# Scaled scores copied out of the score banks, and the second unit's mask moved into the next step

## The chip, the cores and the metric

The kernel runs on one core of a Trainium2 chip. The metric is the device time of one execution in microseconds, the median of several runs.

## The reference

Three layers follow each other, all in float32: a sparse attention (4 batches, 8 heads, 576 tokens, head dimension 64), a gated feed-forward layer (512 to 1536 and back), and a second one with a softmax-like activation and a layer norm (512 to 1024 and back). The change concerns the attention alone:

```python
scores = scale * np.matmul(q, k.transpose(0, 1, 3, 2))
thresh = np.max(scores, axis=-1, keepdims=True) - tau
scores = np.where(scores >= thresh, scores, -1000000000.0)
scores = scores - np.max(scores, axis=-1, keepdims=True)
attn = np.exp(scores)
attn = attn / (np.sum(attn, axis=-1, keepdims=True) + 1e-09)
return np.matmul(attn, v).astype(np.float32)
```

## The kernel before, in words

**Stages.** `attention` runs first, `moe1` (the gated layer, three matmuls for each product of float32 split in two parts) second, `moe2` third. While the attention runs, weights of the second stage are loaded and converted from float64 in pieces: six operations a piece, one on ScalarE (L121), three on VectorE (L125, L128, L131), one on ScalarE (L135), one on GpSimd (L138). The functions `fill` and `conv_emit` place them one by one into the steps.

**Units.** The heads are taken in 16 pairs. A pair has nine units of 128 rows of scores by 576 columns: units 0 to 7 are the four blocks of 128 queries of each of the two heads, unit 8 holds the last 64 queries of both heads, and its scores take twice as many matmuls. A score tile `ps` fills two banks of PSUM, 288 columns in each; the pool `ps_s` has two such tiles.

**What a unit goes through.** `scores` (L277): matmuls into `ps`. `soft_max` (L283): VectorE reads `ps`, multiplies by minus the scale and takes the minimum along the row, `nm`; the elementwise result goes to `junk`, which nobody reads. `soft_exp` (L295): ScalarE reads `ps` again and writes exp(scale * score + nm) to `pe` (unit 8: `pet`). `soft_thr` (L300): GpSimd makes the threshold `th` from `nm` and tau. `soft_mask` (L309): VectorE reads `ps` a third time, compares it with `th`, multiplies into `pe` in place, and sums the row into `z`. One step later `tpose` (L329) transposes the masked unit on TensorE into a tile `tp`, and ScalarE evacuates it (L322). Later `pv` (L360) multiplies with V in four halves per pair, two of 256 and two of 322 columns. `tpose_tail` (L345, L348) transposes the last 64 columns into another tile `tq` of the tag `tp`, `finish` (L381) the reciprocals of the row sums, also into a tile of that tag; it has three buffers. ScalarE evacuates that one into `zt` (L386), and P·V into `xp` (L368).

**The order of the work** is written out by hand. Each engine takes its instructions in the order in which the program issues them. The loop over `m` takes two units a step, A and B (`cur`), and those of the step before (`old`). The string `PROG`, 'ABtVFTUYaufbz', gives the order: A and B are scores, maximum and exponential of the two units; t and u the thresholds; V the P·V matmuls that are due; F `finish`; T and U the transposes of the two old units; Y their tails; a and b the masks; f and z fillers (reciprocals of row sums in `lo_old`, then weight conversions). At the end of the step come DMAs and ScalarE's evacuations: P·V and `zt` first, then those of T, U and Y, then weight conversions. Nine units against two a step make the pattern repeat every nine steps, two pairs. One step of nine has no P·V matmuls; one has both a `finish` and a tail. The last units are in step 71; steps 71 and 72 begin with `prep_x`, which prepares the first block of the second stage on VectorE (L199 and L202).

A score tile comes free when the mask has read it, so scores of a step wait for the masks of the step before:

```python
nc.tensor.matmul(ps[rows, g, 0:HS], lhsT=q[r, u, c], rhs=k[r, u, o:o + HS], start=True, stop=True, skip_group_check=True)
...
nc.vector.scalar_tensor_tensor(out=pv, in0=ps[:, :, 0:HS], scalar=th, in1=pv, op0=ALU.is_ge, op1=ALU.mult, accum_out=z[:, s:s + 1])
```

Of the kernel before, what the change touches and what calls it, by code (L numbers as in the profile page):

```python
# [8 lines left out]
F32 = mybir.dt.float32  # L9
F32R = mybir.dt.float32r  # L10
BF16 = mybir.dt.bfloat16
U32 = mybir.dt.uint32
U64 = mybir.dt.uint64
AF = mybir.ActivationFunctionType
ALU = mybir.AluOpType
AX = mybir.AxisListType
PSUM = bass.MemoryType.PSUM
P = 128
# [3 lines left out]
def kernel(  # L22
# [11 lines left out]
    nc = tc.nc  # L34
    NP, _, VS, D = v.shape
# [11 lines left out]
    HS = S // 2  # L47
# [9 lines left out]
    SCALE = 1.0 / float(D) ** 0.5  # L57
    BIG = 3.0e38
    EPS = 1e-9
    NS = 2 * NQ + 1  # L60
# [11 lines left out]
    taub = const.tile([P, 1], F32, name="taub")  # L72
    neg = const.tile([P, 1], F32, name="neg")
    toff = const.tile([P, 1], F32, name="toff")
# [144 lines left out]

    def tau_consts():  # L220
        nc.vector.tensor_scalar(out=neg, in0=taub, scalar1=0.0, scalar2=None, op0=ALU.is_lt)
        nc.vector.tensor_scalar(out=taub, in0=taub, scalar1=-1.0 / SCALE, scalar2=None, op0=ALU.mult)
        nc.vector.scalar_tensor_tensor(out=toff, in0=neg, scalar=BIG, in1=taub, op0=ALU.mult, op1=ALU.add)

    def attention():
        es = ExitStack()
# [2 lines left out]
        pp = es.enter_context(tc.tile_pool(name="pp", bufs=3))  # L229
# [5 lines left out]
        st = {}  # L235
# [42 lines left out]
            st[i, s] = ps  # L278

        def soft_max(i, s, nm):  # L280
            ps = st[i, s]
            junk = pp.tile([P, 2, HS], BF16, name="junk", bufs=1)
            nc.vector.tensor_scalar(out=junk, in0=ps[:, :, 0:HS], scalar1=-SCALE, scalar2=None, op0=ALU.mult, op1=ALU.min, accum_out=nm)  # L283
            st[i, s] = (ps, nm)

        def soft_exp(i, s):
            ps, nm = st[i, s]
            if s < 2 * NQ:
                qc, h = divmod(s, 2)
                if h == 0:  # L290
                    st[i, "p", qc] = pp.tile([P, 2, S], F32, name="pe", bufs=4)
                pe = st[i, "p", qc][:, h]
            else:
                pe = pp.tile([P, S], F32, name="pet", bufs=2)
            nc.scalar.activation(out=pe.rearrange("p (g s) -> p g s", g=2), in_=ps[:, :, 0:HS], func=AF.Exp, bias=nm, scale=SCALE)  # L295
            st[i, s] = [ps, pe, nm]

        def soft_thr(nm):
            th = sm.tile([P, 1], F32, name="th")
            nc.gpsimd.tensor_scalar(out=th, in0=nm, scalar1=-1.0 / SCALE, scalar2=toff, op0=ALU.mult, op1=ALU.add)  # L300
            return th

        def soft_mask(i, s, th):
            ps, pe, _ = st[i, s]
            if s == 0:
                st[i, "z"] = sm.tile([P, NS], F32, name="z", bufs=2)
            z = st[i, "z"]
            pv = pe.rearrange("p (g s) -> p g s", g=2)
            nc.vector.scalar_tensor_tensor(out=pv, in0=ps[:, :, 0:HS], scalar=th, in1=pv, op0=ALU.is_ge, op1=ALU.mult, accum_out=z[:, s:s + 1])  # L309
            st[i, s] = pe  # L310

        def recip(i):
            rz = sm.tile([P, NS], F32, name="rz", bufs=2)
            z = st[i, "z"]
            lo_q.append(lambda: nc.vector.tensor_scalar(out=rz, in0=z, scalar1=EPS, scalar2=None, op0=ALU.add))
            lo_q.append(lambda: nc.vector.reciprocal(out=rz, in_=rz))
            st[i, "rz"] = rz
# [98 lines left out]
                        conv_emit(wstage, "APD", 2)  # L416

        conv_at = [x for x in range(6, tot // 2 + 6) if x % 2 == 0 or x >= tot // 2]
        PROG = 'ABtVFTUYaufbz'
        for m in range(tot // 2 + 6):  # L420
            if m == tot // 2 - 10:
                load_x(0)
# [2 lines left out]
            cur = [divmod(n, NS) for n in (2 * m, 2 * m + 1) if n < tot]  # L425
# [4 lines left out]
            nm = {}  # L430
            th = {}
# [9 lines left out]
                if k < len(cur):  # L441
                    th[k] = soft_thr(nm[k])

            def mask(k):
                if k < len(cur):
                    soft_mask(*cur[k], th[k])
                    if cur[k][1] == NS - 1:
                        recip(cur[k][0])

            def turn(k):  # L450
                if k < len(old):
                    tpose(*old[k])

            for ch in PROG:
                if ch in "AB":
                    score("AB".index(ch))
                elif ch == "V":
                    for mm in mms:
                        mm()
                elif ch == "F":  # L460
                    for j in range(NP):
                        if m - j * NS // 2 == 9:
                            finish(j)
                elif ch in "TU":
                    turn("TU".index(ch))
                elif ch == "Y":
                    for c in old:
                        tpose_tail(*c)
                elif ch in "tu":
                    thr("tu".index(ch))  # L470
                elif ch in "ab":
                    mask("ab".index(ch))
                elif ch == "f":
                    fill(1)
                elif ch == "z":
                    fill(max(1, len(lo_old)))
# [4 lines left out]
            i, s = divmod(2 * m, NS)  # L481
# [312 lines left out]
```

## Time and profile before

| what | value |
| --- | --- |
| median of 3 runs | 994.72 us (992.99 to 995.31) |
| the profiled execution: its own time | 994.94 us |
| the profiled execution: span from first to last instruction | 993.2 us |
| mean granted TensorE clock | 0.997 |
| TensorE matmuls busy | 958.6 us, 97% of the span |
| VectorE busy | 552.1 us, 56% |
| ScalarE busy | 461.8 us, 47% |
| GpSimd busy | 196.1 us, 20% |

The page counts an engine as busy while one of its instructions executes; in the views below PE is TensorE's matmuls, PEld its weight loads, DVE is VectorE, ACT is ScalarE, POOL is GpSimd. Times are microseconds from the start of the span, those of single instructions in group views nanoseconds. "[1.15 <-DVE pe L309]" behind an instruction says that its engine stood idle for 1.15 us before it and what ended the wait. The shares are means over three stages: the attention fills about the first third of the span, and only there are VectorE and ScalarE busy for most of the time.

### The profile page before, as it was taken

How to read it: one execution, taken by the hardware profiler on the slowest of the kernel's cores; microseconds unless marked ns; L12 is line 12 of the kernel's file. 1: busy time of each engine (PE TensorE's matmuls, PEld its weight loads, DVE VectorE, ACT ScalarE, POOL GpSimd, SP SyncE). 2: the span in 40 equal slices, each digit the busy share in tenths (PEclk: the TensorE clock that was granted, in tenths of full speed). 3: DMA queues.
4: the chain of work that ended last, by engine and by line, in shares of the span. 5: the costliest groups of instructions: out<-in, count | busy, mean ns of one | idle time of the engine just before them, and what ended most of it. 6: DMA issues, size and time to landing. Idle time of an engine off the chain costs nothing.

```text
span 993.2 us, 17033 instructions
## 1 busy us (share of the span) xinstructions
PE 958.6 (97%) x6464; PEld 797.9 (80%) x6464; DVE 552.1 (56%) x1262; ACT 461.8 (47%) x889; POOL 196.1 (20%) x294
## 2 busy tenths in 40 slices
PE   6999898999899999999999999999999999999997
PEld 3555555555558999999999999999999788888885
DVE  5888888877887665553222666322322544444443
ACT  4777777777775444443222444211221434333332
POOL 1111112111113311220000333000001233333331
PEclk9999999999999999999999999999999999999999
DMA  5423532432615655444210554222102111111100
GB/s 140 143 85 96 157 103 84 132 96 82 165 59 176 204 169 155 142 134 122 92 49 24 179 156 154 72 73 72 47 26 94 32 50 47 46 49 45 44 22 32
DMA packets 56002, 95.59 MB, mean 96 GB/s; under 512 B 15088, under 2 KB 33648, under 8 KB 55920
## 3 DMA queue, kind: packets, MB, share of 16 engines
q1 hardware_dynamic: 55488, 93.91, 31.0%
q8 instruction: 51, 0.84, 0.4%
q10 hardware_dynamic: 432, 0.59, 0.2%
q14 instruction: 31, 0.25, 0.1%
HBM read 70.80 MB, written 23.68 MB: 95 GB/s over the span
## 4 chain that ended last, share of the span: by engine, by line
PE 83%; DVE 10%; issue 2%; ACT 2%; DMA 1%; POOL 1%; SPq 0%; DVEq 0%; ACTq 0%
PE ps L542 29%; PE py L564 15%; PE po L698 10%; PE ps L646 9%; PE ps L277 7%; PE po L360 7%; PE tp L329 5%; DVE junk L283 3%; DVE pe L309 2%; PE pl L679 1%; DVE pet L309 1%; PE tq L345 1%; DMA wraw<-in_w_dram 1%; DMA k<-in_qkv_dram 1%; DVE w L131 0%
## 5 line engine op out<-in xcount | busy, mean ns | idle before, releaser
L542 PE MATMUL ps<-xt,w 128*128 128x288 f32 x2304 | 321.4, 295 | 0.3 <-DVE g L549 0.2
L542 PEld LDWEIGHTS ps<-xt,w 128*128 128x128 f32 x2304 | 310.9, 188 | 0.7 <-DVE g L549 0.7
L564 PE MATMUL py<-gt,w 128*128 128x288 f32 x1152 | 168.1, 295 | 0.0
L564 PEld LDWEIGHTS py<-gt,w 128*128 128x128 f32 x1152 | 158.0, 188 | 0.0
L549 DVE TENSOR_TENSOR g<-ps,a 128x288 f32<-128x288 f32 x96 | 43.8, 457 | 192.7 <-ACT a L548 192.7
L138 POOL TENSOR_TENSOR w<-w,w 128x512 fp32r<-128x512 f32 x52 | 77.9, 1498 | 289.9 <-ACT w L135 289.9
L283 DVE TENSOR_SCALAR_CACHE_REDUCE junk<-ps 128x576 bf16<-128x576 f32 x144 | 109.0, 757 | 43.2 <-PE ps L277 34.5
L277 PE MATMUL ps<-k,q 64*128 64x288 f32 (+1 forms) x640 | 105.8, 450 | 25.7 <-DVE pe L309 15.8
L548 ACT ACTIVATE a<-ps 128x288 f32<-128x288 f32 x96 | 39.3, 409 | 187.3 <-PE ps L542 187.3
L295 ACT ACTIVATE pe<-ps,nm 128x576 f32<-128x576 f32 x128 | 94.8, 743 | 66.3 <-DVE junk L283 65.3
L698 PE MATMUL po<-w,lt 128*128 128x512 f32 x432 | 104.5, 395 | 2.6 <-ACT lt L684 1.3
L309 DVE SCALAR_TENSOR_TENSOR pe<-ps,th,pe 128x576 f32<-128x576 f32 x128 | 104.0, 816 | 5.0 <-POOL th L300 3.2
L646 PE MATMUL ps<-w,ys 128*128 128x512 f32 x432 | 105.2, 398 | 1.3 <-POOL ys L518 1.3
L698 PEld LDWEIGHTS po<-w,lt 128*128 128x128 f32 x432 | 80.4, 187 | 23.6 <-ACT lt L684 2.2
L277 PEld LDWEIGHTS ps<-k,q 64*128 64x128 f32 (+1 forms) x640 | 47.3, 179 | 62.3 <-issue 26.4
L646 PEld LDWEIGHTS ps<-w,ys 128*128 128x128 f32 x432 | 79.6, 187 | 20.3 <-POOL ys L518 1.7
L322 ACT ACTIVATE pt<-tp 128x512 f32<-128x512 f32 (+1 forms) x160 | 79.0, 552 | 7.7 <-PE tp L329 5.8
L300 POOL TENSOR_SCALAR th<-nm,toff 128x1 f32<-128x1 f32 x144 | 38.1, 265 | 216.3 <-DVE junk L283 214.2
L360 PE MATMUL po<-pt,vr 128*64 128x322 f32 (+1 forms) x512 | 78.3, 427 | 0.1
L329 PEld LDWEIGHTS tp<-ident,pe 128*128 128x128 f32 x512 | 58.0, 145 | 24.8 <-issue 17.4
L329 PE MATMUL tp<-ident,pe 128*128 128x128 f32 x512 | 72.9, 285 | 0.9 <-ACT pt L322 0.9
L551 DVE TENSOR_TENSOR gt<-g,gt 128x288 fp32r<-128x288 f32 x96 | 44.0, 458 | 49.1 <-ACT gt L550 49.1
(73 smaller groups left out, 802.3 us busy)
## 6 DMA issues: line engine op xcount, KB each, us to landing
wraw<-in_w_dram SPq DMA_DIRECT2D x36, 512.0 KB
q<-in_qkv_dram SPq DMA_DIRECT2D x15, 576.0 KB
k<-in_qkv_dram SPq DMA_DIRECT2D x30, 176.0 KB
xd<-xp SPq DMA_DIRECT2D x16, 289.0 KB
xr<-xd SPq DMA_DIRECT2D x8, 576.0 KB
zr<-rzd SPq DMA_DIRECT2D x16, 288.0 KB
xsd<-xr SPq DMA_DIRECT2D x8, 576.0 KB
ypd<-y SPq DMA_DIRECT2D x8, 576.0 KB
```

What stands on the lines that cost most here:

```text
L138: nc.gpsimd.tensor_tensor(out=w["o"][1], in0=w["f"] if wide else raw, in1=w["o"][0].bitcast(F32), op=ALU.subtract)
L277: nc.tensor.matmul(ps[rows, g, 0:HS], lhsT=q[r, u, c], rhs=k[r, u, o:o + HS], start=True, stop=True, skip_group_check=True)
L283: nc.vector.tensor_scalar(out=junk, in0=ps[:, :, 0:HS], scalar1=-SCALE, scalar2=None, op0=ALU.mult, op1=ALU.min, accum_out=nm)
L295: nc.scalar.activation(out=pe.rearrange("p (g s) -> p g s", g=2), in_=ps[:, :, 0:HS], func=AF.Exp, bias=nm, scale=SCALE)
L309: nc.vector.scalar_tensor_tensor(out=pv, in0=ps[:, :, 0:HS], scalar=th, in1=pv, op0=ALU.is_ge, op1=ALU.mult, accum_out=z[:, s:s + 1])
L322: evac_q.append(lambda: nc.scalar.activation(out=out, in_=in_, func=AF.Copy))
L329: nc.tensor.transpose(tp[:, kc, :], pe[:, o:o + P], ident)
L360: nc.tensor.matmul(po[h * D:(h + 1) * D], lhsT=lhsT, rhs=rhs, start=(kc == 0), stop=(kc == NQ), skip_group_check=True)
L542: nc.tensor.matmul(pa[:, 0:NB], lhsT=wt[:, m, wi, kc * P:(kc + 1) * P], rhs=xt[:, kc, xi, :], start=(k == 0), stop=(k == 3 * KC - 1))
L564: nc.tensor.matmul(py, lhsT=wt[:, 2, wi, oc * P:(oc + 1) * P], rhs=gt[:, gi, :], start=(first and k == 0), stop=(last and k == 2))
L646: nc.tensor.matmul(ph[:, g, :], lhsT=y[:, a, kc, :], rhs=w2(2 * kc + g, b), start=(k == 0), stop=(k == 3 * KC - 1))
L698: nc.tensor.matmul(po, lhsT=lt[:, a, j, :], rhs=w2(2 * KC + j, b), start=(k == 0), stop=(k == 3 * NJ - 1))
```

## The change

`soft_max` writes its elementwise result, minus the scaled scores, as float32 to a tile `ns` in SBUF with four buffers, in place of `junk`. `soft_exp` and `soft_mask` read `ns`, so nothing but the maximum reads `ps`. The threshold is compared on the negative scaled scores, so the constants of `tau_consts` and the comparison turn round, and one operation on 128 x 1 elements goes. The order of a step becomes 'AtbBuVFTUYfaz': b, the mask of unit B, is put off into a list `late` and done in the next step, behind that step's first maximum and before its second. The first filler now stands ahead of mask A.

```diff
@@ -219,8 +219,7 @@
 
     def tau_consts():
         nc.vector.tensor_scalar(out=neg, in0=taub, scalar1=0.0, scalar2=None, op0=ALU.is_lt)
-        nc.vector.tensor_scalar(out=taub, in0=taub, scalar1=-1.0 / SCALE, scalar2=None, op0=ALU.mult)
-        nc.vector.scalar_tensor_tensor(out=toff, in0=neg, scalar=BIG, in1=taub, op0=ALU.mult, op1=ALU.add)
+        nc.vector.scalar_tensor_tensor(out=toff, in0=neg, scalar=-BIG, in1=taub, op0=ALU.mult, op1=ALU.add)
 
     def attention():
         es = ExitStack()
@@ -278,13 +277,12 @@
             st[i, s] = ps
 
         def soft_max(i, s, nm):
-            ps = st[i, s]
-            junk = pp.tile([P, 2, HS], BF16, name="junk", bufs=1)
-            nc.vector.tensor_scalar(out=junk, in0=ps[:, :, 0:HS], scalar1=-SCALE, scalar2=None, op0=ALU.mult, op1=ALU.min, accum_out=nm)
-            st[i, s] = (ps, nm)
+            ns = pp.tile([P, 2, HS], F32, name="ns", bufs=4)
+            nc.vector.tensor_scalar(out=ns, in0=st[i, s][:, :, 0:HS], scalar1=-SCALE, scalar2=None, op0=ALU.mult, op1=ALU.min, accum_out=nm)
+            st[i, s] = (ns, nm)
 
         def soft_exp(i, s):
-            ps, nm = st[i, s]
+            ns, nm = st[i, s]
             if s < 2 * NQ:
                 qc, h = divmod(s, 2)
                 if h == 0:
@@ -292,21 +290,21 @@
                 pe = st[i, "p", qc][:, h]
             else:
                 pe = pp.tile([P, S], F32, name="pet", bufs=2)
-            nc.scalar.activation(out=pe.rearrange("p (g s) -> p g s", g=2), in_=ps[:, :, 0:HS], func=AF.Exp, bias=nm, scale=SCALE)
-            st[i, s] = [ps, pe, nm]
+            nc.scalar.activation(out=pe.rearrange("p (g s) -> p g s", g=2), in_=ns, func=AF.Exp, bias=nm, scale=-1.0)
+            st[i, s] = (ns, pe)
 
         def soft_thr(nm):
             th = sm.tile([P, 1], F32, name="th")
-            nc.gpsimd.tensor_scalar(out=th, in0=nm, scalar1=-1.0 / SCALE, scalar2=toff, op0=ALU.mult, op1=ALU.add)
+            nc.gpsimd.tensor_scalar(out=th, in0=nm, scalar1=1.0, scalar2=toff, op0=ALU.mult, op1=ALU.add)
             return th
 
         def soft_mask(i, s, th):
-            ps, pe, _ = st[i, s]
+            ns, pe = st[i, s]
             if s == 0:
                 st[i, "z"] = sm.tile([P, NS], F32, name="z", bufs=2)
             z = st[i, "z"]
             pv = pe.rearrange("p (g s) -> p g s", g=2)
-            nc.vector.scalar_tensor_tensor(out=pv, in0=ps[:, :, 0:HS], scalar=th, in1=pv, op0=ALU.is_ge, op1=ALU.mult, accum_out=z[:, s:s + 1])
+            nc.vector.scalar_tensor_tensor(out=pv, in0=ns, scalar=th, in1=pv, op0=ALU.is_le, op1=ALU.mult, accum_out=z[:, s:s + 1])
             st[i, s] = pe
 
         def recip(i):
@@ -416,7 +414,8 @@
                         conv_emit(wstage, "APD", 2)
 
         conv_at = [x for x in range(6, tot // 2 + 6) if x % 2 == 0 or x >= tot // 2]
-        PROG = 'ABtVFTUYaufbz'
+        PROG = 'AtbBuVFTUYfaz'
+        late = []
         for m in range(tot // 2 + 6):
             if m == tot // 2 - 10:
                 load_x(0)
@@ -441,11 +440,10 @@
                 if k < len(cur):
                     th[k] = soft_thr(nm[k])
 
-            def mask(k):
-                if k < len(cur):
-                    soft_mask(*cur[k], th[k])
-                    if cur[k][1] == NS - 1:
-                        recip(cur[k][0])
+            def mask(c, t):
+                soft_mask(*c, t)
+                if c[1] == NS - 1:
+                    recip(c[0])
 
             def turn(k):
                 if k < len(old):
@@ -468,8 +466,14 @@
                         tpose_tail(*c)
                 elif ch in "tu":
                     thr("tu".index(ch))
-                elif ch in "ab":
-                    mask("ab".index(ch))
+                elif ch == "a":
+                    if cur:
+                        mask(cur[0], th[0])
+                    if len(cur) > 1:
+                        late.append((cur[1], th[1]))
+                elif ch == "b":
+                    while late:
+                        mask(*late.pop())
                 elif ch == "f":
                     fill(1)
                 elif ch == "z":

```

## Rows read from the trace of the kernel before

**Rows 1.** Busy time by stretch; behind the engines: granted TensorE clock, DMA share, GB/s.

```profile
235.00:240.00 5.00, 5.00 (x26) 3.14 (x26) 3.15 (x9) 2.92 (x6) 0.53 (x2) 0.66 0.00 0
...
400.00:600.00 200.00, 200.00 (x1508) 200.00 (x1507) 88.81 (x174) 73.12 (x157) 28.65 (x18) 1.00 0.36 115
```

**Rows 2.** Waits, 8 to 306 us: who waited for whom, total us, times, longest.

```profile
PE ps L277 <- DVE pe L309: 15.8, 20, 1.7
...
PE ps L277 <- DVE pet L309: 2.9, 8, 0.6
```

**Rows 3.** Timeline, step without P·V: start, us, engine, line, operation [idle before].

```profile
46.33 1.24 PE L277 MATMUL ps<-k,q 64*128 64x288 f32 x8
...
47.14 0.76 DVE L283 TENSOR_SCALAR_CACHE_REDUCE junk<-ps 128x576 bf16<-128x576 f32 x1 [1.11 <-PE ps L277]
...
47.94 0.74 ACT L295 ACTIVATE pe<-ps,nm 128x576 f32<-128x576 f32 x1 [0.88 <-DVE junk L283]
...
48.03 0.76 DVE L283 TENSOR_SCALAR_CACHE_REDUCE junk<-ps 128x576 bf16<-128x576 f32 x1
...
48.78 0.82 DVE L309 SCALAR_TENSOR_TENSOR pe<-ps,th,pe 128x576 f32<-128x576 f32 x1
...
49.75 0.76 PE L277 MATMUL ps<-k,q 64*128 64x288 f32 x4 [1.15 <-DVE pe L309]
```

**Rows 4.** Timeline of TensorE, L348 in steps with a `finish`, six cycles apart.

```profile
46.07 0.34 PE L348 MATMUL tq<-ident,pet 128*64 128x64 f32 x4
...
267.97 0.34 PE L348 MATMUL tq<-ident,pet 128*64 128x64 f32 x4
```

**Rows 5.** The chain that ended last, 66 to 83 us: start, us, what.

```profile
66.66 1.17 PE ps L277 x8
...
67.83 1.24 PE po L360 x8
...
69.06 1.02 PE tp L329 x8
...
71.65 1.78 PE po L360 x12
...
74.46 0.22 PE tq L345 x2
...
79.68 1.45 PE po L360 x12
```

**Rows 6.** Timeline of TensorE and ScalarE in a step with L381 and a tail.

```profile
79.61 1.08 PE L360 MATMUL po<-pt,vr 128*64 128x256 f32 x8
...
80.52 0.74 ACT L295 ACTIVATE pe<-ps,nm 128x576 f32<-128x576 f32 x1 [0.20 <-DVE junk L283]
...
81.48 0.25 ACT L386 ACTIVATE zt<-rt 9x128 f32<-9x128 f32 x1
...
82.05 0.38 PE L345 MATMUL tq<-ident,pe 128*128 128x128 f32 x2
```

**Rows 7.** Timeline of TensorE: a score pair whose first unit is split.

```profile
74.60 1.40 PE L277 MATMUL ps<-k,q 64*128 64x288 f32 x12
```

**Rows 8.** One source line each: ns min/median/max, first and last start (L138: 8 to 304 us).

```profile
L199 DVE SCALAR_TENSOR_TENSOR xr<-xr,vs,zr x32: 509/511/1565, 296.4 to 493.4; 128x288 f32<-128x288 f32 x32
...
L309 DVE SCALAR_TENSOR_TENSOR pe<-ps,th,pe x128: 808/817/820, 9.9 to 300.8; 128x576 f32<-128x576 f32 x128
...
L131 DVE SCALAR_TENSOR_TENSOR w<-w,wlow x52: 682/685/1593, 57.2 to 621.1; 128x512 uint32<-128x512 uint32 x52
...
L138 POOL TENSOR_TENSOR w<-w,w x12: 1267/1280/1284, 59.6 to 297.7; 128x512 fp32r<-128x512 f32 x12
```

**Rows 9.** Groups of ScalarE: busy us, mean ns of one, idle before, releaser.

```profile
L548 ACT ACTIVATE a<-ps 128x288 f32<-128x288 f32 x96 | 39.3, 409 | 187.3 <-PE ps L542 187.3
...
L550 ACT ACTIVATE gt<-g 128x288 fp32r<-128x288 f32 x96 | 42.7, 445 | 54.3 <-DVE g L549 54.3
```

**Rows 10.** Timeline of VectorE at the end of the attention.

```profile
302.44 1.42 DVE L202 TENSOR_TENSOR xt<-xr,xt 128x576 fp32r<-128x576 f32 x2
```

## The prediction

> **What bounds the kernel now.** I first asked for busy time by stretch. From 400 to 600 us TensorE is busy for the whole 200 us [rows 1], and so it is nearly to the end: what the change does to VectorE can win nothing in the two dense layers. The attention, about 8 to 307 us, is left. There I read the list of waits: TensorE sits 15.8 us on `pe` and 2.9 us on `pet`, both written by VectorE's mask at L309 [rows 2]. These are the score matmuls (L277), which need one of two score banks, and a bank is free only when its mask has read it. These 18.7 us are what the change is after.
>
> The timeline of one step without P·V matmuls shows the wait. Scores A start at 46.33, the first row maximum at 47.14 (0.81 later), the second at 48.03, mask A at 48.78, and the scores of the next step stand 1.15 us until that mask is through [rows 3]. VectorE goes maximum, maximum, mask, mask.
>
> The order repeats every nine steps (two head pairs). Its mark is the small tail matmul L348 in the step that also holds a `finish`: the one at 46.07 and the one at 267.97 are six cycles apart [rows 4], so a cycle takes 221.90 / 6 = 36.98 us, a step 4.11.
>
> **TensorE's own work in a cycle**, from pieces of the chain that stand without a wait: 1.17 for a score pair, 1.24 and 1.78 for the halves of the wide P·V, 1.45 for the second half of the narrow one, 1.02 for the two transposes, 0.22 for a tail [rows 5]; 1.08 for the narrow first half [rows 6]; 0.26 for L348, from 46.07 to 46.33 [rows 3, 4]; a score pair with the split last unit 1.40 less an overlap of some 0.06 [rows 7]. Sum: 7 x 1.17 + 2 x 1.34 + 2 x (1.08 + 1.45 + 1.24 + 1.78) + 9 x 1.02 + 4 x 0.22 + 2 x 0.26 = 32.55. So 4.43 us of a cycle are waits or slow matmuls. Part is the clock: between 235 and 240 the granted clock is 0.66 [rows 1]. Between the two levels of 2.4 and 1.2 GHz that is 68% of 5 us at the lower one, 1.7 us of work lost; one more such fall stands between 195 and 205, so 2 x 1.7 / 6 = 0.57 a cycle.
>
> **The change, part by part.**
>
> *Bank released by the maximum.* The exponential and the mask now read `ns`, so scores of the next step need only that a maximum is done, over 2 us earlier than TensorE comes to them. The bank waits go to nothing.
>
> *What is late next: mask B.* It is done in the next step between the two maxima, and the transposes of unit B stand behind it. From rows: maximum A starts 0.81 after the scores, the next operation of another kind 0.75 later (48.03 to 48.78), mask 0.82, and 0.15 to reach TensorE (mask A from 48.78 to 49.60, scores at 49.75) [rows 3]: 0.80 + 0.75 + 0.82 + 0.15 = 2.52. With a P·V half between, TensorE is at these transposes after 1.17 + 1.08 + 0.51 = 2.76 or later: hidden. In the one step of nine without P·V it is there after 1.68 and waits 0.84.
>
> *What is late as well: the exponential of B.* Maximum B now starts 2.29 after the scores instead of 1.70, its exponential 0.80 after that (47.14 to 47.94 for unit A [rows 3]), at 3.09. Behind it in ScalarE's queue stand the evacuations. In the one step of nine that has both the reciprocals' transpose (L381) and a tail, the tail takes a fourth buffer of `tp`, of which there are three, so it needs the evacuation `zt`. That starts 0.96 after the exponential and takes 0.25 [rows 6]: 3.09 + 0.98 + 0.25 + 0.15 = 4.47. TensorE would be there at 1.17 + 2.44 (79.61 to 82.05) = 3.61 and waits 0.86. Elsewhere the tail finds a buffer evacuated a step ago.
>
> *VectorE's own step*: four operations of alternating kinds at 0.75, 3.00, against 0.89 + 0.75 + 0.89 + 0.75 now, the second 0.89 being mask B's wait for its exponential (48.03 + 0.80 + 0.74 + 0.10 is 49.67, 0.89 after 48.78 [rows 3]). Three weight conversions (0.69 us each at most) for each of 12 pieces [rows 8] are 0.37 a step over 67 steps. 3.37 is under TensorE's 32.55 / 9 = 3.62, so what hides VectorE's work is thin, 0.25 a step.
>
> *Operations with another operand.* The maximum writes float32 instead of bfloat16: taken at nothing, at most the 0.06 by which a mask exceeds it, and hidden by that cover. The exponential reads SBUF: a ScalarE copy of 288 elements takes 445 from SBUF and 409 ns from PSUM [rows 9], so +0.04, in ScalarE's idle time except for the 0.02 that stand in the 0.98 above. The mask now has two SBUF sources. The nearest row is L199, the same kind of operation, float32, with a pointer scalar, two SBUF sources and no accumulator: 511 ns for 288 elements against 817 for 576 with one source in PSUM [rows 8]. That is 1.06 ns for each further element, one rate for both, so I take no change.
>
> The Trainium skill (Vector Engine (DVE) Microarchitecture Reference, section 7, Points that are easy to get wrong) says that this form with two SBUF sources that are not bfloat16 runs at half throughput, for want of a port for the accumulator. By that rule the sum would end slower, which is the third rival below; L199 with its 511 ns does not show it, but no row here has accumulator and two SBUF sources together.
>
> *Contention with GpSimd.* L199 and L131, with two SBUF sources, have maxima of 1565 and 1593 ns beside medians of 511 and 685; the mask with one in PSUM never exceeds 820 [rows 8]. The long ones stand beside a running L138 on GpSimd. After the change the mask is of the first kind, and 12 L138 fall into the attention. Each can cost from nothing to 1.05 us (1565 less 511): 0 to 12.6, taken at half of that, -6, since a held mask A has time to spare and a held mask B has little.
>
> *The threshold and the constants.* Same count on GpSimd; one tiny operation less before the first maximum, off the path: nothing. The reciprocal of odd pairs moves by a step and shifts weight conversions by a step; its reader is four steps away. No DMA moves past another on any queue.
>
> *Start.* The first three steps with transposes have no P·V either. Each can trade a wait like the 1.15 [rows 3] for the new 0.84, and the first may lose it whole: between 0 (K's arrival and slow first matmuls stand close behind) and 1.15 + 2 x 0.31 = 1.8, taken at +1.0.
>
> *End.* The last mask B now comes in a step that begins with two L202 subtractions (1.42 us [rows 10]), in front of it on VectorE; the last transposes and P·V wait for it. Between 0 and 3 with one conversion more in the last steps, taken at -1.2.
>
> **Sum.** A cycle falls from 36.98 to 32.55 + 0.84 + 0.86 + 0.57 = 34.82, by 2.16; steps 4 to 70 are 7.4 cycles: 16.0. 16.0 - 6 + 1.0 - 1.2 = 9.8. The profiled execution took 994.94, 0.2 above the median of 994.72; it gives 985.1, the median 984.9: I say 985.0.
>
> **The rivals.**
> 1. *The clock.* Both falls follow a step in which TensorE waited over a microsecond. The two new waits lie within some 5 us of each other in each cycle. If the clock falls in each, 7.4 x 1.7 = 12.6 instead of 4.2: +8.4, 993.4. For it: the falls. Against: most cycles have such waits now without a fall.
> 2. *GpSimd holds the masks.* Each L138 delays the path by its full 1.28, 15.4 instead of 6, with the next threshold queued behind it on GpSimd: 994.4. For it: the 1565 ns. Against: L138 may meet mask A, which has slack.
> 3. *The mask at half rate* (slower): 576 x 1.06 = 0.61 us more for each mask. VectorE's step becomes 3.00 + 1.22 + 0.37 = 4.59, a cycle 41.3 instead of 36.98: +4.3 x 7.4 = 32, about 1027. It decides from the point where the step exceeds 4.11, 0.37 us more per mask. For it: the accumulator is new beside two SBUF sources. Against: L199.
>
> **How the numbers follow.** Forecast 0.72, rival 1 0.08, rival 2 0.08, rival 3 0.12. A measurement here can tell 0.2%, 2 us, from no change. The forecast is faster; rival 1 is half faster and half the same; rival 2 is 0.02 faster, 0.05 the same, 0.01 slower; rival 3 is slower. Faster 0.78, same 0.09, slower 0.13. The range goes down to 976, all 18.7 us of bank waits gained, and up to 993.5: the contention at its bound (+6.6) with the end at its bound (+1.8), which takes in rival 1 too. Rivals 2 and 3 and a remnant are left out.
>
> **What would show it.** Right: no TensorE wait on L309 before L277; cycles near 35.5; a wait of about 0.85 before unit B's transposes in the step without P·V and one on `zt` before L345; masks at 0.82 except beside L138. Wrong: a mask median near 1.4; the lower clock in each cycle; transposes waiting in steps with P·V, where mask B should be hidden.

## The result, and the profile after

The changed kernel takes 977.24 us (median of 4 runs, 976.68 to 977.84), the kernel before 993.93 (4 runs, 992.99 to 995.31): a ratio of 0.9831 [0.9814, 0.9848], 16.7 us less. The forecast was 985.0, from 976.0 to 993.5. The profiled execution took 976.86 us with a span of 975.1, so the two spans differ by 18.1 us where the working came to 9.8: the sign was right, and the size little more than half of what came. A second execution of the kernel before, profiled later, has a span of 991.7 us, 16.6 more than the changed kernel, which is the difference of the medians; what made the first longer is under *The clock*.

Part 5 of the page after, the groups of the attention:

```profile
L281 DVE TENSOR_SCALAR_CACHE_REDUCE ns<-ps 128x576 f32<-128x576 f32 x144 | 108.4, 752 | 35.3 <-PE ps L276 34.9
L293 ACT ACTIVATE pe<-ns,nm 128x576 f32<-128x576 f32 x128 | 98.6, 775 | 57.5 <-DVE ns L281 57.0
L298 POOL TENSOR_SCALAR th<-nm,toff 128x1 f32<-128x1 f32 x144 | 86.1, 600 | 154.7 <-DVE ns L281 144.6
L307 DVE SCALAR_TENSOR_TENSOR pe<-ns,th,pe 128x576 f32<-128x576 f32 x128 | 105.1, 821 | 5.4 <-POOL th L298 5.4
...
L276 PE MATMUL ps<-k,q 64*128 64x288 f32 (+1 forms) x640 | 95.7, 439 | 4.6 <-DMA k<-in_qkv_dram 4.6
```

The scores (now L276) wait for K's transfer at the very beginning and for nothing else: the 18.7 us of [rows 2] are gone. Before the maximum (L281) VectorE waits for TensorE. The mask takes 821 ns on average, the same as before [rows 8]; what has grown is a GpSimd operation on 128 x 1 elements, the threshold (L298), from a mean of 264 to 600 ns.

What TensorE waits for after, in the list of waits from 8 to 290 us (us in total, times, longest):

```profile
PE tq L343 <- ACT zt L384: 6.6, 8, 1.5
PE tp L327 <- ACT pe L293: 5.4, 8, 1.0
PE tp L327 <- DVE pe L307: 2.1, 2, 1.5
PE tp L327 <- DVE pet L307: 0.8, 1, 0.8
```

Two of these were forecast, each once in a cycle of nine steps. The timeline of the changed kernel shows one such place:

```profile
41.09 0.25 ACT L384 ACTIVATE zt<-rt 9x128 f32<-9x128 f32 x1
...
41.39 0.44 PE L343 MATMUL tq<-ident,pe 128*128 128x128 f32 x2 [0.53 <-ACT zt L384]
...
41.76 0.34 PE L346 MATMUL tq<-ident,pet 128*64 128x64 f32 x4
...
42.02 1.24 PE L276 MATMUL ps<-k,q 64*128 64x288 f32 x8
...
42.83 0.76 DVE L281 TENSOR_SCALAR_CACHE_REDUCE ns<-ps 128x576 f32<-128x576 f32 x1 [1.98 <-PE ps L276]
...
43.20 0.66 PE L327 MATMUL tp<-ident,pe 128*128 128x128 f32 x4
...
43.51 0.82 DVE L307 SCALAR_TENSOR_TENSOR pe<-ns,th,pe 128x576 f32<-128x576 f32 x1
...
43.76 0.69 POOL L298 TENSOR_SCALAR th<-nm,toff 128x1 f32<-128x1 f32 x1 [2.79 <-DVE ns L281]
...
44.25 0.76 DVE L281 TENSOR_SCALAR_CACHE_REDUCE ns<-ps 128x576 f32<-128x576 f32 x1
...
44.48 0.63 PE L327 MATMUL tp<-ident,pe 128*128 128x128 f32 x4 [0.63 <-ACT pe L293]
...
45.04 1.24 PE L276 MATMUL ps<-k,q 64*128 64x288 f32 x8
...
248.55 0.34 PE L346 MATMUL tq<-ident,pet 128*64 128x64 f32 x4
```

The eight score matmuls of the next step now stand in one stretch of 1.24 us (45.04); before, they came as two groups of four, the first behind a wait of 1.15 [rows 3]. VectorE goes maximum (42.83), old mask B (43.51), maximum (44.25). TensorE waits until 44.48 for that mask, which ended at 44.33; the list names `pe` of ScalarE, which had long been done (the exponential in the same tile, 40.15 to 40.93), so the name is to be read with the timeline. From the mark at 41.76 to the one at 248.55 are six cycles: 206.79 / 6 = 34.47 us, against 36.98 [rows 4].

The busy time over six cycles splits that. First the changed kernel (stretch, its length, TensorE's matmuls busy, then weight loads, VectorE, ScalarE, GpSimd, granted clock, DMA):

```profile
41.76:248.55 206.79, 197.69 (x1501) 119.58 (x1500) 176.95 (x488) 162.33 (x310) 77.03 (x118) 1.00 0.39 118
```

then the same stretch of the fastest kernel of the study (with `ns`, old order of the masks, `finish` moved, below):

```profile
40.50:235.87 195.37, 195.37 (x1501) 119.64 (x1500) 177.45 (x486) 160.10 (x308) 41.01 (x118) 1.00 0.43 126
```

There TensorE has no gap at all: 195.37 / 6 = 32.56 us of work in a cycle; the forecast had 32.55 from single pieces. The changed kernel stands idle for 206.79 - 197.69 = 9.10 us, 1.52 a cycle (six waits on `zt` of 4.5 us together, six for mask B of 4.6), and its matmuls take 197.69 - 195.37 = 2.32, or 0.39 a cycle, longer. 32.56 + 1.52 + 0.39 = 34.47.

### The profile page after: what moved, and what is told of

It is laid out like the page before. It is cut to its first block, busy times and chain, and to the rows that moved or that the text cites. A ratio compares the mean times of both kernels' runs of the same rounds, so it can differ in the third digit from the quotient of the medians.

```text
span 975.1 us, 16895 instructions
## 1 busy us (share of the span) xinstructions
PE 948.0 (97%) x6464; PEld 798.6 (82%) x6464; DVE 539.7 (55%) x1261; ACT 460.2 (47%) x889; POOL 246.7 (25%) x294
## 4 chain that ended last, share of the span: by engine, by line
PE 90%; DVE 3%; ACT 2%; issue 2%; DMA 1%; SPq 1%; POOL 0%; ACTq 0%; DVEq 0%
PE ps L546 31%; PE py L568 16%; PE po L702 10%; PE ps L650 9%; PE po L358 8%; PE ps L276 8%; PE tp L327 6%; PE pl L683 1%; ACT pe L293 1%; PE tq L343 1%; DMA q<-in_qkv_dram 1%; DVE pe L307 1%; DMA k<-in_qkv_dram 0%; PE tq L346 0%; DVE e L658 0%
## 5 line engine op out<-in xcount | busy, mean ns | idle before, releaser
L138 POOL TENSOR_TENSOR w<-w,w 128x512 fp32r<-128x512 f32 x52 | 80.7, 1553 | 282.7 <-ACT w L135 277.3
L281 DVE TENSOR_SCALAR_CACHE_REDUCE ns<-ps 128x576 f32<-128x576 f32 x144 | 108.4, 752 | 35.3 <-PE ps L276 34.9
L293 ACT ACTIVATE pe<-ns,nm 128x576 f32<-128x576 f32 x128 | 98.6, 775 | 57.5 <-DVE ns L281 57.0
L298 POOL TENSOR_SCALAR th<-nm,toff 128x1 f32<-128x1 f32 x144 | 86.1, 600 | 154.7 <-DVE ns L281 144.6
L307 DVE SCALAR_TENSOR_TENSOR pe<-ns,th,pe 128x576 f32<-128x576 f32 x128 | 105.1, 821 | 5.4 <-POOL th L298 5.4
L276 PE MATMUL ps<-k,q 64*128 64x288 f32 (+1 forms) x640 | 95.7, 439 | 4.6 <-DMA k<-in_qkv_dram 4.6
L276 PEld LDWEIGHTS ps<-k,q 64*128 64x128 f32 (+1 forms) x640 | 48.2, 178 | 29.1 <-issue 9.8
```

The costliest lines, as they stand in the source:

```text
L138: nc.gpsimd.tensor_tensor(out=w["o"][1], in0=w["f"] if wide else raw, in1=w["o"][0].bitcast(F32), op=ALU.subtract)
L281: nc.vector.tensor_scalar(out=ns, in0=st[i, s][:, :, 0:HS], scalar1=-SCALE, scalar2=None, op0=ALU.mult, op1=ALU.min, accum_out=nm)
L298: nc.gpsimd.tensor_scalar(out=th, in0=nm, scalar1=1.0, scalar2=toff, op0=ALU.mult, op1=ALU.add)
L307: nc.vector.scalar_tensor_tensor(out=pv, in0=ns, scalar=th, in1=pv, op0=ALU.is_le, op1=ALU.mult, accum_out=z[:, s:s + 1])
```

## The experiments

**The two halves of the change.** First: `ns`, but the masks in the order of before.

```diff
-        PROG = 'AtbBuVFTUYfaz'
+        PROG = 'ABtVFTUYaufbz'
@@
-                    if len(cur) > 1:
-                        late.append((cur[1], th[1]))
                 elif ch == "b":
-                    while late:
-                        mask(*late.pop())
+                    if len(cur) > 1:
+                        mask(cur[1], th[1])
```

> Only the first half of the change: scaled scores in `ns`, but the order of a step as before (maximum, maximum, mask, mask, all in the unit's own step). Theory 1, the bank release carries the gain and the late mask opens two new waits (about 0.63 us on mask B in the step without P·V and 0.73 us on `zt` in the step with `finish` and tail, some 10 us in all): neither wait is there, VectorE's step is about 3.2 us (mask B waits for its exponential) plus 0.4 of fillers against TensorE's 3.6, so 972 to 982 us. Rival, the alternation is needed because VectorE's step would be the bound without it: 984 to 990 us, with score matmuls or transposes waiting on VectorE in most steps.

965.43 us (964.41 to 966.24), ratio 0.9713 [0.9695, 0.9731], less than either range expected; a cycle is 32.98 us. The copy outside the banks gains 28 us by itself, and moving the mask gives 12 of them back. TensorE's waits on `zt` shrink to 1.4 us in 3, and those for mask B in the step without P·V are gone.

Second: the mask moved, but read from the score banks as before.

```diff
-        PROG = 'ABtVFTUYaufbz'
+        PROG = 'AtbBuVFTUYfaz'
+        late = []
@@ the loop over ch
+                elif ch == "a":
+                    if cur:
+                        mask(cur[0], th[0])
+                    if len(cur) > 1:
+                        late.append((cur[1], th[1]))
+                elif ch == "b":
+                    while late:
+                        mask(*late.pop())
```

> Only the second half: scores stay in the banks, mask B is done in the next step between the two maxima. Theory 1: unit B's bank is now held until 2.4 us after the next step's first scores, scores B wait for that and maximum B behind them, so a step is about 4.9 us instead of 4.1: 1035 to 1055 us. Rival, the order by itself shortens VectorE's step from 3.3 to 3.0 and so gains: 980 to 988 us.

1155.29 us (1155.01 to 1161.78), ratio 1.1639 [1.1604, 1.1675]: the sign was as expected, the loss some three times as large. TensorE and VectorE in this kernel's timeline, and the windows from 8 to 464 us, nearly all of its attention:

```profile
156.18 0.76 DVE L283 TENSOR_SCALAR_CACHE_REDUCE junk<-ps 128x576 bf16<-128x576 f32 x1 [0.33 <-PE ps L277]
...
156.87 0.81 DVE L309 SCALAR_TENSOR_TENSOR pe<-ps,th,pe 128x576 f32<-128x576 f32 x1
...
157.83 0.76 PE L277 MATMUL ps<-k,q 64*128 64x288 f32 x4 [1.69 <-DVE pe L309]
158.52 1.08 PE L360 MATMUL po<-pt,vr 128*64 128x256 f32 x8
...
161.47 0.76 PE L277 MATMUL ps<-k,q 64*128 64x288 f32 x4
162.27 0.76 DVE L283 TENSOR_SCALAR_CACHE_REDUCE junk<-ps 128x576 bf16<-128x576 f32 x1 [1.94 <-PE ps L277]
```

```profile
8.00:464.00 456.00, 331.21 (x1928) 182.42 (x1928) 236.73 (x638) 219.00 (x398) 55.77 (x154) 0.86 0.23 70
```

Scores B need the bank that mask B holds, and mask B now stands behind maximum A, so TensorE waits about 1.7 us in most steps (97.5 us in 57 waits). Everything else of the step (P·V, transposes) is queued behind those scores and can no longer fill the wait: the old order had that work in front of it. The waits are not the whole loss: the granted clock averages 0.86 over these 456 us, which is 0.14 x 456 = 64 us of work lost, and in the kernel's four runs it is 0.944 to 0.950 over the span. The expectation had no term for that. A late mask pays only once the mask has left the banks.

**The two new waits.** One was taken away by `finish` of even pairs in step 10 instead of 9, away from the tail:

```diff
-                        if m - j * NS // 2 == 9:
+                        if m - j * NS // 2 == (9 if j % 2 else 10):
```

> The kernel after, with `finish` of the even pairs one step later, in the step without P·V and without a tail, so that no tail needs a fourth buffer of `tp`. Theory 1, the wait of L343 on `zt` (6.6 us in eight waits in the trace of after) is on the path: 970 to 972 us, and no wait on `zt`. Rival, what is saved there comes back as a longer wait for mask B in the next step: 976 to 978 us.

969.03 us (968.91 to 969.13), ratio 0.975 [0.9734, 0.9765]: 8.2 us less than the changed kernel, 1 more than expected, and no wait on `zt` is left in the list.

The other by doing mask B in its own step where a step without P·V follows:

```diff
                         late.append((cur[1], th[1]))
+                        if m % NS == 0:
+                            mask(*late.pop())
```

> The kernel after, with mask B done in its own step (behind mask A) in the one step of nine whose successor has no P·V. Theory 1, the late mask costs a wait of 0.63 us in each such successor (eight of them): 971.5 to 973.5 us, and the second transposes there no longer wait. Rival, VectorE's own time behind mask A is on the path there, so the wait only moves: 976 to 978 us.

971.29 us (970.71 to 972.89), ratio 0.9776 [0.9748, 0.9804], 5.9 us less; the wait put down to `pe` L293 falls from 5.4 to 1.7 us. Both waits cost more than their idle time. In the six cycles the first edit saves 6.7 us (206.79 to 200.08) and the second 5.6 (to 201.23), where 4.5 and 4.6 us of idle time stood. Of this 0.7 and 0.95 are matmuls that take less time again. The first edit also takes 1.5 us from the waits for mask B (4.6 to 3.1; the longest, 1.45, is gone).

Both together, with the block of the second stage behind the last mask (the edit of the end, below):

> The changed kernel with three of the earlier edits together: the finish of even pairs one step later, the second mask in its own step when the step without P.V follows (m a multiple of nine), and the second block of the second stage prepared behind the last late mask. Theory 1 (the two waits are separate terms of the sum): the gains of the two edits measured alone, 8.2 and 5.9 us, add to 14.1, so 963 us (between 961 and 965), as fast as the old order of masks with ns and the finish moved (963.4). Theory 2 (a late mask also loses time by a fuller VectorE queue and by GpSimd waiting beside running masks): it stays some 4 us or more behind, 966 to 970.

966.93 us (966.3 to 967.8), ratio 0.9732 [0.9715, 0.9748]. The gains don't add (10.3 instead of 14.1). In the six cycles they could not: 6.7 and 5.6 are more than the 206.79 - 195.37 = 11.4 us that there was to gain. The cycle is down to 197.39 / 6 = 32.90, still 0.34 above TensorE's own work, and at the end the last L379 waits 2.7 us for an evacuation. The time is the one that theory 2 gave; whether VectorE's queue is the reason, as it says, no run shows.

The masks in the old order with `ns`, and `finish` moved:

> Scaled scores in `ns` with the old order, and `finish` of the even pairs in the step without P·V. The wait on `zt` is 1.4 us in three waits there. Theory 1, with the exponentials early nothing else is late: 963 to 965 us, 0.5 to 1.5 less than with the old order alone. Rival, the buffer of `tp` taken in the next step by `finish` waits for an evacuation instead: 965 to 967 us.

963.44 us (963.05 to 963.8), ratio 0.9692 [0.967, 0.9714]: the fastest kernel of the study. Its cycles are those of the second windows line above: in them TensorE waits for nothing.

**Contention with GpSimd.** The low parts of the weights converted during the attention are set to zero by VectorE, without GpSimd:

```diff
-            nc.gpsimd.tensor_tensor(out=w["o"][1], ..., op=ALU.subtract)
+            if k < 3 * FW:
+                nc.vector.memset(w["o"][1].bitcast(F32), 0.0)
+            else:
+                nc.gpsimd.tensor_tensor(out=w["o"][1], ..., op=ALU.subtract)
```

> The kernel after; the low parts of the weights converted during the attention are set to zero on VectorE instead of being computed by L138 on GpSimd (this leaves out their share of the result). So no long GpSimd operation meets a mask in the attention. If the contention costs what the prediction took, 6 us: 970 to 972 us. If the longer masks are absorbed by VectorE's spare time, as most of the trace of after suggests: 975 to 977.5 us.

976.23 us (975.99 to 976.97), ratio 0.9824 [0.9805, 0.9844]: 1.0 us less than the changed kernel, inside the interval. The contention is not worth 6 us. (The edit gives VectorE a `memset` of 0.49 us a piece instead; the six cycles take 205.90 us, 0.9 less.) What it does is in the timeline of the changed kernel:

```profile
85.05 1.44 POOL L138 TENSOR_TENSOR w<-w,w 128x512 fp32r<-128x512 f32 x1 [1.92 <-ACT w L135]
...
86.78 0.82 DVE L307 SCALAR_TENSOR_TENSOR pe<-ns,th,pe 128x576 f32<-128x576 f32 x1 [0.73 <-POOL th L298]
...
146.20 1.27 POOL L138 TENSOR_TENSOR w<-w,w 128x512 fp32r<-128x512 f32 x1 [2.42 <-ACT w L135]
...
146.45 1.64 DVE L307 SCALAR_TENSOR_TENSOR pe<-ns,th,pe 128x576 f32<-128x576 f32 x1
...
148.24 0.63 PE L327 MATMUL tp<-ident,pe 128*128 128x128 f32 x4 [1.45 <-DVE pe L307]
```

and in the rows by source line (ns, min/median/max):

```profile
L307 DVE SCALAR_TENSOR_TENSOR pe<-ns,th,pe x128: 803/815/1635, 9.3 to 279.1; 128x576 f32<-128x576 f32 x128
...
L298 POOL TENSOR_SCALAR th<-nm,toff x144: 256/692/1291, 8.1 to 279.3; 128x1 f32<-128x1 f32 x144
```

with the threshold's row in the kernel before:

```profile
L300 POOL TENSOR_SCALAR th<-nm,toff x144: 264/264/268, 8.3 to 301.0; 128x1 f32<-128x1 f32 x144
```

Whichever starts second is held here. At 146.20 L138 is first: the mask at 146.45 takes 1.64 us, and as it is a mask B in a step without P·V, TensorE waits 1.45 instead of 0.63. That happens to 1 of the 128 masks, the maximum of the row. Of the eleven L138 up to 262 us the other ten start beside a running mask and take 1.38 to 1.70, as the 1.44 at 85.05, against 1.27 for the one at 146.20. The threshold is held likewise: its median is 692 ns against 264 before, and at 43.76 it starts beside the mask that ends at 44.33 and ends at 44.45. The delayed threshold then holds a mask A (0.73 at 86.78), which has time to spare.

**VectorE's spacing.** Before, two maxima start 0.89 apart and a maximum and a mask 0.75 [rows 3]. The forecast put that down to kind. The kernel before with a second `junk` buffer:

```diff
-            junk = pp.tile([P, 2, HS], BF16, name="junk", bufs=1)
+            junk = pp.tile([P, 2, HS], BF16, name="junk", bufs=2)
```

> The kernel before, with two buffers for `junk` instead of one. In before the second maximum starts 0.89 us after the first, in the old order with `ns` (four buffers) 0.68. Theory 1, the one shared buffer makes the second maximum wait for the first to be written: 0.68 here too, and where the score banks' wait is on the path it shortens by up to 0.2 us a step: 983 to 990 us. Rival, the gap belongs to two accumulating operations of one kind in a row: 0.89 stays and the time is that of before, 992 to 995 us.

VectorE's timeline of this kernel:

```profile
45.97 0.76 DVE L283 TENSOR_SCALAR_CACHE_REDUCE junk<-ps 128x576 bf16<-128x576 f32 x1 [1.05 <-PE ps L277]
...
46.65 0.75 DVE L283 TENSOR_SCALAR_CACHE_REDUCE junk<-ps 128x576 bf16<-128x576 f32 x1
...
47.62 0.82 DVE L309 SCALAR_TENSOR_TENSOR pe<-ps,th,pe 128x576 f32<-128x576 f32 x1 [0.20 <-ACT pe L295]
```

Two maxima of the same kind now start 0.68 apart. The 0.21 had come from the shared buffer, not from the kind: in the trace of before 72 of the 144 maxima wait for a semaphore of VectorE's own, here and in the changed kernel none does, so it is a wait that the program asks for. The 0.75 between a maximum and mask A fits a wait too, for mask A's own exponential (47.94 + 0.74, and the 0.10 of the forecast's working, is 48.78 [rows 3]); the changed kernel has 0.68 there (42.83 to 43.51). The kernel gains little all the same, 990.89 us, between the two ranges expected (10 runs, 989.32 to 992.48), ratio 0.997 [0.9958, 0.9981]: mask A now waits 0.20 for its exponential, and the waits for banks stay (18.5 us against 18.7).

**The end.** The second block of the second stage is prepared behind the last late mask:

```diff
-            if 0 <= m - tot // 2 + 1 < 2:
-                prep_x(0, m - tot // 2 + 1)
+            if m == tot // 2 - 1:
+                prep_x(0, 0)
@@ behind the masks in "b"
+                    if m == tot // 2:
+                        prep_x(0, 1)
```

> The kernel after, with the two L202 subtractions of step 72 behind the last mask B instead of in front of it. Theory 1, they hold the last transposes and P·V, as predicted for 1.2 us and as the trace of after suggests for more: 974 to 976 us. Rival, VectorE's and ScalarE's chain of weight conversions sets the end of the attention, whichever comes first: 977 to 978 us.

978.21 us (977.01 to 978.55), ratio 0.9838 [0.9815, 0.9861]: no gain. In the changed kernel's timeline, two waits follow each other:

```profile
279.83 1.42 DVE L202 TENSOR_TENSOR xt<-xr,xt 128x576 fp32r<-128x576 f32 x2
...
281.18 0.81 DVE L307 SCALAR_TENSOR_TENSOR pet<-ns,th,pet 128x576 f32<-128x576 f32 x1
...
282.14 0.63 PE L327 MATMUL tp<-ident,pet 128*128 128x128 f32 x4 [0.78 <-DVE pet L307]
...
282.63 0.63 ACT L135 ACTIVATE w<-w 128x512 fp32r<-128x512 f32 x1 [1.67 <-DVE w L131]
...
283.99 0.25 ACT L384 ACTIVATE zt<-rt 9x128 f32<-9x128 f32 x1
...
284.29 0.44 PE L343 MATMUL tq<-ident,pe 128*128 128x128 f32 x2 [1.52 <-ACT zt L384]
```

The edit takes the first (0.78) away, and the second grows to 2.74, as this kernel's timeline shows:

```profile
284.45 0.44 PE L343 MATMUL tq<-ident,pe 128*128 128x128 f32 x2 [2.74 <-ACT zt L384]
```

So it is not L202 alone that sets the end. ScalarE stands 1.67 us for a weight conversion that VectorE does behind its masks, and `zt` is queued behind it. So the conversions were taken out of that step:

```diff
-        conv_at = [x for x in range(6, tot // 2 + 6) if x % 2 == 0 or x >= tot // 2]
+        conv_at = [x for x in range(6, tot // 2 + 6) if (x % 2 == 0 or x >= tot // 2) and x != tot // 2]
```

> The changed kernel without weight conversions in the first step that has no new unit (the 73rd, m = 72); they follow later. Theory 1 (at the end VectorE's and ScalarE's conversion, with ScalarE's evacuation of zt behind the operation that waits for it, holds the last transposes): the wait of 1.5 us on zt before the last L343 goes or falls under 0.5, the last L379 comes 1 to 2.5 us earlier, and so does the end: 975 to 976 instead of 977.2. Theory 2 (what holds the last steps is the late mask with the exponential before it): the last transposes keep their waits and the time stays within 1 us of 977.2.

975.88 us (974.17 to 976.8), ratio 0.9816 [0.9799, 0.9834]. And with the edit before:

> The same, and the second block of the second stage prepared behind the last late mask. Theory 1: with both of its causes gone (0.8 us before the last unit's transposes, 1.5 us on zt) the end gains 2 to 4 us, 973 to 975. Theory 2: no more than 1 us from 977.2. A third case: the last L379 comes earlier, but the first matmul of the second stage then waits for its prepared block, and the time stays.

976.15 us (975.12 to 976.37), ratio 0.9823 [0.9808, 0.9837]. In both the wait on `zt` is gone, and the last L379 comes at 286.84 and 285.63 instead of 289.71; but the time falls by no more than 1.4 and 1.1 us, within the intervals. TensorE's timeline in the last one, and its granted clock behind it (the windows):

```profile
285.63 0.28 PE L379 MATMUL rt<-ident,rz 128*9 128x128 f32 x1
...
294.05 4.97 PE L548 MATMUL ps<-xt,w 128*128 128x288 f32 x24 [1.75 <-DVE g L555]
```

```profile
292.00:300.00 8.00, 6.25 (x36) 6.01 (x35) 5.47 (x11) 4.22 (x9) 2.57 (x2) 0.79 0.91 250
```

The second stage begins 4 us earlier and then waits 1.75 us for VectorE's gate `g`, behind which the granted clock averages 0.79 over 8 us, part of it at the lower of the two levels (0.21 x 8 = 1.7 us of work lost). This is near the third case of the expectation, though the wait is for the gate and not for the prepared block: what the attention's end gains, the next stage gives back. In the trace of the run with only the conversions out, part of it goes so: that wait is 0.69 us at a granted clock of 1.00, the second stage gives back 1.2 of the 2.9 us, and the rest goes in the third stage, where the clock falls between 958 and 962 us, a fall that the changed kernel's trace does not have there.

**The clock.** The kernel before, unchanged, with a second profile.

> The kernel before, unchanged, with a second profile. Theory 1 (the falls of TensorE's granted clock in the attention belong to this kernel's schedule): they stand again at 190 to 210 and 230 to 240 us, at 0.83 to 0.94 in these slices. Theory 2 (they differ from execution to execution): they stand elsewhere or are missing, the cycle of nine steps then averages 36.98 less up to 0.57 us, and the term for the clock was no property of the kernel.

993.5 us, with a span of 991.7. The windows of its attention:

```profile
190.00:200.00 10.00, 8.53 (x65) 5.49 (x63) 8.45 (x24) 7.24 (x16) 1.07 (x4) 1.00 0.25 79
...
230.00:240.00 10.00, 8.40 (x59) 4.63 (x62) 8.41 (x22) 8.11 (x15) 2.62 (x6) 1.00 0.12 46
```

and of its six cycles:

```profile
45.36:264.57 219.21, 203.77 (x1502) 118.40 (x1501) 185.67 (x486) 163.94 (x310) 41.67 (x118) 1.00 0.38 111
```

The granted clock is 1.00 where it fell in [rows 1], and each cycle is 0.45 us shorter: 219.21 / 6 = 36.53. These falls differ from execution to execution. Without them a cycle of before has 219.21 - 203.77 = 15.44 us, 2.57 a cycle, of idle time, and matmuls that are (203.77 - 195.37) / 6 = 1.40 longer.

## Why the forecast was right, and too small

| term | forecast, us | measured, us | against the second execution of before |
| --- | --- | --- | --- |
| TensorE's own work in a cycle | 32.55 | 32.56 | |
| idle at both new waits in a cycle | 0.84 + 0.86 | 0.77 + 0.75 | |
| longer matmuls beside them | none | 0.39 | |
| lower clock in a cycle after | 0.57 | 0 | |
| cycle after | 34.82 | 34.47 | |
| cycle before | 36.98 | 36.98 | 36.53 |
| 7.4 cycles, gain | 16.0 | 18.6 | 15.3 |
| contention | -6 | in the line above, -1 at most | the same |
| start | +1.0 | +3.8 | +3.1 |
| end, as what is left of the sum | -1.2 | -4.3 | -1.8 |
| sum | 9.8 | 18.1 | 16.6 |

The last column is the one to judge by: the trace from which the forecast starts has two falls of the clock in its cycles, and neither the second execution of before nor the changed kernel has one there. Against it the cycles gain (219.21 - 206.79) / 6 = 2.07 each, where the forecast had 2.16.

*Bank released by the maximum*: right. The waits of [rows 2] are gone, and their going is worth more than their 18.7 us, 28 in the run with the old order. Beside the idle time each wait also broke the matmuls' overlap: eight score matmuls take 1.24 us in one stretch, and four after a wait 0.76 [rows 3]. In all the matmuls of a cycle of before take 1.40 us longer at full clock. The forecast took this from the difference of cycle and work rather than from the list of waits, so it holds.

*Mask B and the exponential of B*: right in place and cause. One undisturbed wait is 0.63, 0.84 forecast. VectorE lets the transposes go 2.46 us after the scores (42.02 to 44.48) instead of 2.52, as the maximum and the mask start 0.68 apart, not 0.75. And TensorE comes to them 1.83 us after the scores (43.85) instead of 1.68: the four transposes of unit A take 0.66 by themselves, not half of the 1.02 of eight. The wait on `zt` is 4.5 us in the six cycles, 0.75 each (0.86 forecast). Over the six cycles the idle time came out 0.18 a cycle less than forecast and the matmuls beside it 0.39 longer, which the sum did not have; that the two misses partly cancel is luck. Taking them away alone gave 5.9 and 8.2 us. In steps with P·V mask B is hidden, as worked out.

*The clock*: wrong as a term. "one more such fall stands between 195 and 205, so 2 x 1.7 / 6 = 0.57 a cycle" took one execution's falls for a property of the schedule. The second execution of before has none in its six cycles; the changed kernel has none either, though TensorE stands idle for 1.52 us of each. So rival 1 falls for this change. Since 36.98 holds such falls too, the term stood on both sides of the difference and cost the forecast little. That falls never come of waits is not shown: the clock of the kernel with the late mask alone averages 0.86, and at the end of the attention it falls in every trace that keeps the wait on `zt` there (see *End*).

*Contention*: the term that was most mis-sized. "taken at half of that, -6" held that the 12 L138 hold masks, and half of their time falls on masks that matter. One mask of 128 was held, because the mask is mostly running first and GpSimd waits. That is rival 2 the other way round, and it costs 1 us at most (the run without L138). The sign "cycles near 35.5" had this term in it and came out at 34.47.

*Operations with another operand*: right. The exponential takes 775 ns instead of 743, +0.03. For the mask, the rule of the Trainium skill (Vector Engine (DVE) Microarchitecture Reference, section 7, Points that are easy to get wrong) does not show: with accumulator and two float32 SBUF sources the median is 815 ns, with one source in PSUM 817 [rows 8]. So rival 3 falls.

*Start*: "between 0 ... and 1.8, taken at +1.0" was too small. TensorE's score matmuls in the first steps, before and after:

```profile
10.85 2.30 PE L277 MATMUL ps<-k,q 64*128 64x288 f32 x8 [1.69 <-DVE pe L309]
...
22.38 1.61 PE L277 MATMUL ps<-k,q 64*64 64x288 f32 x12 [0.73 <-DVE pe L309]
```

```profile
5.86 4.95 PE L276 MATMUL ps<-k,q 64*128 64x288 f32 x14 [0.51 <-DMA k<-in_qkv_dram]
...
18.61 1.40 PE L276 MATMUL ps<-k,q 64*64 64x288 f32 x12
```

Scores of the second step stood 1.69 us for the bank at 10.85; now they run in one stretch with the first step's, and the fifth step (its unit split into 64 x 64) begins at 18.61 instead of 22.38. What was thought to stand close behind, K, had arrived. Of the 3.8 us 2.0 are idle time, 0.2 are K's earlier arrival, and 1.6 are matmuls: the eight score matmuls at 10.85 take 2.30 us, while in the changed kernel eight take 1.24 from 12.37 on. Why the first matmuls of either kernel are slow, no run shows. The run with the old order of the masks begins its fifth step at 18.46, so it is the copy that gives this gain.

*End*: "Between 0 and 3 ..., taken at -1.2" was near in size, by the last column, but its cause was in good part another. That row is what is left of the sum (16.6 - 15.3 - 3.1), and so holds all that lies behind the cycles; the nearness is luck. The attention's end costs more, and 2.7 us are made up behind it: from the last finish to the end of the span the second execution of before takes 688.1 us, the changed kernel 685.4. From the last mark (267.97 before [rows 4], 248.55 after) to the last finish (L381 at 306.97 before, L379 at 289.71 after) the changed kernel needs 2.2 us more. What holds it is the chain of conversions, with `zt` behind it, more than L202, and the granted clock falls behind that wait. It does so in all four traces that keep the wait (this one, and those of L138 left out, mask B in time and L202 moved); in the two without the conversions it is 1.00 there:

```profile
284.50:290.00 5.50, 5.46 (x29) 4.25 (x28) 4.51 (x5) 3.09 (x8) 2.92 (x3) 0.69 0.51 151
```

Against the second execution of before the misses are -0.7 (the cycles, with what contention there is inside them), +6.0 (contention), +2.1 (start) and -0.6 (end): 6.8 together, from 9.8 to 16.6. The forecast was too small by the contention and the start. The other 1.5 us of the 18.1 are the first execution's own.

## What to carry to other kernels

A buffer shared by two stages can cost more than the waits that the trace lists, as the overlap of TensorE's matmuls breaks at each (here 18.7 us in the list, 28 gained); measure the work of an undisturbed cycle and take the difference. Profile the starting kernel twice before a difference of two traces is put down to the change: one execution here held 0.45 us a cycle that the next did not have. Do the two halves of a change one by one: the copy out of the banks was worth 28 us, and the reordering that it made possible took 12 of them back. A gain at the end of one stage counts only as far as the next stage's inputs are ready.

## What the runs showed of the hardware

- A row maximum of 128 x 576 elements on VectorE starts 0.21 us later behind another one when both write the same buffer than when they write different ones (0.89 against 0.68). With the one buffer the second waits for a semaphore of VectorE's own.
- A GpSimd operation on 128 x 1 elements takes 692 ns instead of 264 when it starts beside a running VectorE mask with two SBUF sources; before, where 71 of them started beside masks with one source in PSUM, none took more than 268. The Trainium skill (GPSIMD Engine Reference, section 1, Specifications) says that GpSimd shares its SBUF interfaces with VectorE and contends with instructions that have two SBUF inputs; the trace agrees, and the one that started second waited, GpSimd here as VectorE at 146.45.
- The spread of the kernel before goes with the clock: its runs at a mean granted clock of 1.000 took 991.5 to 992.5 us, those at 0.998 took 992.7 to 994.5, one at 0.993 took 997.85.
